# A two-layer linear-attention and MLP block on one core: output tiles in the phi(K) buffers, two more normalised tiles, a last tile cut 384 + 128, and new operation lists

## The chip, the core and the metric

The kernel runs on one NeuronCore of one Trainium2 chip. Five engines work from their own instruction lists: TensorE (PE: matmuls, with the weight loads shown as PEld), VectorE (DVE), ScalarE (ACT), GpSimd (POOL) and SyncE (SP), which here only issues DMAs. They meet through semaphores. The metric is the device time in microseconds; the median of three runs before the change is 328.74 us (328.71 to 331.37).

## The reference

The input x has 2048 tokens of 512 values. Two layers follow each other with the same weights, each with an attention part and an MLP part, and each part is added to its input:

```python
phi = lambda t: jnp.where(t > 0, t + 1, jnp.exp(t)) + 1e-6
# A: H = 32 heads of 16; q, k, v = split(x @ wqkv)
pq, pk = phi(q), phi(k)
kv = jnp.einsum("bhsd,bhse->bhde", pk, v)
z = jnp.einsum("bhsd->bhd", pk)
o = einsum("bhqd,bhde->bhqe", pq, kv) / (einsum("bhqd,bhd->bhq", pq, z)[..., None] + 1e-6)
A = o @ wo
# B: F = 1792
h = gelu(layernorm(x) @ w1 + b1);  B = h @ w2 + b2
...
x = x + A(layernorm(x))
x = x + B(layernorm(x))
x = x + A(layernorm(x))
x = x + B(layernorm(x))
```

The sums kv and z run over all tokens, so the attention output of a layer can't begin before all its keys are there.

## The kernel before

The tokens are 16 tiles of 128 (st 0 to 15), four to a chunk (c 0 to 3). `build_kernel` describes the whole computation as a graph of 1541 named operations, each with an engine, a duration that a planner uses, the tiles it holds, and the function that emits its instructions. The order on each engine is not found by the program: it stands written out in `CONF["ORDER"]`, one list of names for each engine. `Scheduler.run` only walks the five lists with the stated durations, to give every tile a buffer and every operation a place in time; `assign_waits` then derives the semaphore waits. So on the chip each engine runs its list strictly in order, and an operation that waits holds up all behind it on that engine. Constants such as the durations matter only through the buffers they lead to and through the lists that were settled with them.

Names: the layer is L (0 or 1).

- `x0`, `x1`, `x2`, `xc0` to `xc2`: DMAs that load x; `wk0`, `wk1`, `wq`: weights. The first layer begins with chunk 3 (tiles 12 to 15).
- `stats`, `aggr`, `veps`, `pow`, `nmr`, `norm` with A or B, layer and tile (L734 to L774): the layer norm. Statistics are on VectorE, `veps` and `pow` (one over the root) mostly on GpSimd, `norm` on VectorE or ScalarE; the result is a tile of `yb`, of which there are 10. In the first chunk, `cen` subtracts the mean and `ysc` scales later.
- `TA`, `TB` (L784): a DMA transpose of a `yb` tile, issued by SP; `PTA`, `PTB` with `tc` (L797, L807): the same on TensorE, copied out by ScalarE.
- `K`, `Q` (L852, L870, L883): projections. `exp`, `relu`, `min`, `phi` (L822 to L839) turn them into phi(K), in eight buffers `pkb`, and phi(Q). `phi` stands on VectorE or GpSimd.
- `G`, then `ga`, `gt` (L985 to L998): the product of normalised tokens and phi(K), summed over chunks; `KV`, `kvm`, `M`, `cpm` (L1008 to L1031): the value and output weights folded in. `Z`, `zs`, `zb`, `dz`, `ZR`, `D`, `pz`, `red`, `den`, `rec`, `pr` (L934, L1053 to L1085): the denominator. `TP` (L1069) transposes phi(Q) when the denominator is taken token by token.
- `WO` and `RA` (L1101, L1106): attention output and residual; `b2` adds the MLP's bias to it (L1118).
- `W1L_c_f_h` (L1133): the up-projection of chunk c for 128 of the 1792 columns, four matmuls of 512 tokens, or for chunk 0 two halves of 256 (last digit 0 or 1); `gelu` (L1139) on ScalarE.
- `W2L_st_0` and `W2L_st_7` (L1171): the down-projection of a tile in two runs of seven matmuls; `RB` (L1177, L1181) its residual.
- `OD` (L1183): the store of a finished tile, issued by SP. In layer 1 `RB` writes it into one of two `outb` buffers. The last tile (st 15) is cut into two halves of 256 columns, `W21_15_h0` and `h1` (L1158), with `RB1_15_0`, `RB1_15_1` (L1163) and `OD15_0`, `OD15_1` (L1165), so that less is left after the last matmul.
- `warm`, `idle0_0`, `idle0_1` (L690): dummy matmuls at the head, 8 of 512 columns and 1 of 128, then 4 and 3 of 128.

TensorE's eight accumulator banks are shared by all these products; `WO` and `W2` use banks 3, 4 and 5. The tail of the last tile before the change:

```python
ot = Tile(OUT, f"out{st}")
for h in range(2):
    hb = b if h == 0 else Tile(psum, f"w{L}_{st}_h", "w")
    cs = slice(h * D // 2, (h + 1) * D // 2)
```

Of the kernel before, what the change touches and what calls it, by code (L numbers as in the profile page):

```python
# [6 lines left out]
BF16 = mybir.dt.bfloat16  # L7
# [20 lines left out]
DMA_LAT = 800.0  # L28

# [81 lines left out]
class Scheduler:  # L111
# [12 lines left out]
    def run(self):  # L124
# [13 lines left out]
        bus = 0.0  # L138
        for _ in g.ops:
# [33 lines left out]
            if e == "pool" and o.sem is None and o.dur > 300.0:  # L173
                dur += max(0.0, min(dve_busy - at, 400.0))
                pool_busy = at + dur
# [92 lines left out]
def assign_waits(graph, order, sems, dma_sems):  # L268
# [10 lines left out]
    while len(done) < total:  # L279
        moved = False  # L280
        for e in ENGINES:
# [43 lines left out]
    N_WARM2=1, N_IDLE=[4, 3], XQ='sp', WKQ='sp act', WK1=1,  # L325
    LAND={'x0': 3210, 'x1': 3930, 'wk1': 5300, 'wk0': 6430, 'x2': 6950, 'wq': 8450, 'xc0': 9730, 'xc1': 11020, 'xc2': 12240},
# [38 lines left out]
        "act":  # L365
# [167 lines left out]
def build_kernel(nc, A_x, A_wqkv, A_wo, B_x, B_w1, B_b1, B_w2, B_b2, out, conf=None, report=False):  # L533
# [5 lines left out]
    with ExitStack() as es:  # L539
        def SB(name, shape, dt):  # L540
            return es.enter_context(nc.sbuf_tensor(name, shape, dt))
# [46 lines left out]
        def bank(t, n=512):  # L588
            return ps[:, t.slot, 0:n]
# [778 lines left out]
```

## Time and profile before

| what | value |
|---|---|
| runs before | 328.71, 328.74, 331.37 us; median 328.74 |
| the profiled execution's own time, its span | 326.2 us, first to last instruction |
| median less span | 2.5 us |
| granted TensorE clock | 1.000 |
| first projection (K0_12) on TensorE | 6.55 us |
| start of the last matmul | 323.38 us |
| output stores: issue to landing, 128 KB and 64 KB | 2.1 and 2.0 us (medians) |
| DMA transposes of yb: issue to landing | 2.5 us (median, 56 of them) |

The page's first part gives the busy time of each engine and the second the span in 40 slices. The waits are a table of who waited for whom: total, times, longest. The chain is the work that ended last, followed back from the end. In a timeline each line is one or several instructions: start, time from the first start to the last end, engine, line, operation, output and input, count, and in brackets the idle time before it and what ended it. Times on TensorE overlap: a 512-column matmul is shown with 0.38 us but the next one starts 0.216 us after it.

### The profile page before, as it was taken

What the parts mean: (1) busy time and instruction counts of PE and PEld (TensorE: products, weight loads), DVE (VectorE), ACT (ScalarE), POOL (GpSimd) and SP (SyncE); (2) the same over time, 40 slices, a digit from 0 to 9 for tenths busy, and PEclk for the clock granted to TensorE, in tenths of its full rate; (3) what the DMA queues carried; (4) which work ended last, traced back from release to release, by engine and by line L of the source; (5) the groups of instructions that cost most, each with busy time, mean ns of one, the idle gap of its engine ahead of it and who ended that gap; (6) DMA issues with size and microseconds to landing.
All of it is one profiled execution on the core that took longest, in us unless ns stands there. A gap on an engine that the chain in (4) does not pass through costs nothing.

```text
span 326.2 us, 4796 instructions
## 1 busy us (share of the span) xinstructions
PE 320.6 (98%) x1724; PEld 158.2 (48%) x1724; DVE 218.7 (67%) x506; ACT 197.5 (61%) x338; POOL 131.2 (40%) x224
## 2 busy tenths in 40 slices
PE   7999999999999999999999999999999999999996
PEld 3444545656544444444444444458644444444453
DVE  4998689989866662535468899999988663300132
ACT  5998889744753387357963395969923553645200
POOL 3465637673238106134139525645811275100000
PEclk9999999999999999999999999999999999999999
DMA  7424662524012400312110200111153233300011
GB/s 239 163 51 92 173 223 62 181 49 81 21 31 48 97 1 2 74 22 55 27 32 19 47 17 0 28 39 36 32 92 72 48 45 69 81 0 2 32 64 50
DMA packets 47028, 20.39 MB, mean 62 GB/s; under 512 B 41948, under 2 KB 45532, under 8 KB 47004
## 3 DMA queue, kind: packets, MB, share of 16 engines
q1 hardware_dynamic: 45676, 15.09, 20.4%
q0 software_dynamic: 1056, 4.72, 4.5%
q10 hardware_dynamic: 272, 0.26, 0.3%
q8 instruction: 14, 0.23, 0.3%
q14 instruction: 10, 0.08, 0.1%
HBM read 8.00 MB, written 2.10 MB: 31 GB/s over the span
## 4 chain that ended last, share of the span: by engine, by line
PE 91%; DVE 4%; DMA 2%; ACT 1%; SPq 1%; issue 1%; ACTq 0%
PE ps L1133 29%; PE ps L1171 26%; PE ps L1101 9%; PE ps L852 9%; PE ps L870 5%; PE ps L953 4%; PE ps L883 3%; PE ps L985 2%; DMA t<-in_A_x_dram 1%; PE ps L1158 1%; DMA t<-yb 1%; DVE t L839 1%; PE ps L1008 1%; PE ps L1077 1%; PE ps L797 1%
## 5 line engine op out<-in xcount | busy, mean ns | idle before, releaser
L1139 ACT ACTIVATE gT<-ps,b1c 128x512 bf16<-128x512 f32 (+1 forms) x140 | 76.9, 601 | 61.2 <-PE ps L1133 60.8
L1133 PE MATMUL ps<-t,w 128*128 128x512 bf16 (+1 forms) x560 | 102.2, 336 | 0.5 <-DMA t<-yb 0.3
L1171 PE MATMUL ps<-w,gT 128*128 128x512 bf16 x434 | 97.3, 379 | 0.0
L1133 PEld LDWEIGHTS ps<-t,w 128*128 128x128 bf16 x560 | 54.4, 98 | 44.5 <-DMA t<-yb 0.7
L1171 PEld LDWEIGHTS ps<-w,gT 128*128 128x128 bf16 x434 | 42.4, 98 | 50.4 <-ACT gT L1139 0.3
L822 ACT ACTIVATE eb<-ps 128x512 bf16<-128x512 f32 x56 | 32.1, 606 | 21.3 <-PE ps L852 20.3
L749 POOL TENSOR_TENSOR rstd<-veps,neghalf 128x1 f32<-128x1 f32 x64 | 36.7, 581 | 8.2 <-DVE veps L747 5.5
L1181 DVE TENSOR_TENSOR outb<-ps,xsb 128x512 bf16<-128x512 f32 x15 | 10.3, 689 | 40.3 <-PE ps L1171 32.1
L734 DVE BATCH_NORM_STATS2 stats<-xsb 128x6 f32<-128x512 f32 x48 | 32.0, 681 | 0.2
L1101 PE MATMUL ps<-gtb,t 128*128 128x512 bf16 x128 | 31.8, 379 | 0.1
L852 PE MATMUL ps<-wqkv,t 128*128 128x512 bf16 x128 | 31.1, 379 | 0.0
L769 ACT ACTIVATE yb<-xsb,nmr,rstd 128x512 bf16<-128x512 f32 x21 | 16.8, 811 | 12.6 <-POOL nmr L766 12.5
L833 ACT ACTIVATE rb<-ps 128x512 bf16<-128x512 f32 x38 | 22.3, 611 | 1.6 <-PE ps L852 0.9
L739 POOL TENSOR_SCALAR veps<-mv 128x1 f32<-128x1 f32 x32 | 7.3, 227 | 38.4 <-DVE mv L736 36.6
L774 DVE TENSOR_SCALAR yb<-xsb,mv,rstd 128x512 bf16<-128x512 f32 x27 | 15.0, 572 | 9.0 <-POOL rstd L749 8.9
L835 DVE TENSOR_SCALAR eb<-eb 128x512 bf16<-128x512 bf16 x46 | 13.6, 306 | 10.9 <-ACT eb L822 10.8
L1118 POOL TENSOR_TENSOR xsb<-xsb,b2b 128x512 f32<-128x512 f32 x14 | 17.0, 1218 | 8.1 <-DVE yb L774 6.5
L870 PE MATMUL ps<-wqkv,t 128*128 128x512 bf16 x80 | 20.2, 379 | 0.0
L747 POOL TENSOR_SCALAR veps<-mv 128x1 f32<-128x1 f32 x28 | 8.4, 305 | 28.0 <-DVE mv L736 26.9
L1101 PEld LDWEIGHTS ps<-gtb,t 128*128 128x128 bf16 x128 | 12.3, 98 | 14.9 <-ACT gtb L966 0.7
L852 PEld LDWEIGHTS ps<-wqkv,t 128*128 128x128 bf16 x128 | 12.0, 97 | 14.7 <-ACT t L807 0.9
L1065 POOL TENSOR_TENSOR t<-t,rr 128x512 bf16<-128x512 bf16 x7 | 7.7, 1100 | 24.4 <-DVE rr L1061 14.1
(103 smaller groups left out, 398.7 us busy)
## 6 DMA issues: line engine op xcount, KB each, us to landing
w<-in_B_w_dram POOLq DMA_DIRECT2D x4, 896.0 KB, 5.9
out_dram<-outb SPq DMA_DIRECT2D x15, 128.0 KB, 2.1
t<-in_A_x_dram SPq DMA_DIRECT2D x3, 512.0 KB, 7.3
t<-yb SPq DMA_TRANSPOSE x56, 2.5
wqkv<-in_A_wqkv_dram SPq DMA_DIRECT2D x1, 512.0 KB, 5.7
wo<-in_A_wo_dram POOLq DMA_DIRECT2D x1, 512.0 KB, 6.6
wqkv<-in_A_wqkv_dram POOLq DMA_DIRECT2D x1, 512.0 KB, 4.5
t<-t SPq DMA_TRANSPOSE x20, 2.5
```

Of the source, the lines that this page charges most:

```text
L734: G.op("dve", lambda e: e.bn_stats(stats[:, s.slot, :], src()), 620, reads=src_keys, writes=[k + "s"], tiles=[s, *src_tiles], prio=prio, n ...
L749: G.op("pool", lambda e: e.tensor_tensor(rstd[:, s.slot:s.slot + 1], veps[:, s.slot:s.slot + 1], neghalf[:], op=ALU.pow), 570, reads=[k + ...
L769: G.op("act", lambda e: e.activation(yb[:, y.slot, :], src(), ACT.Identity, bias=nmr[:, s.slot:s.slot + 1], scale=rstd[:, s.slot:s.slot + 1]),
L822: G.op("act", lambda e: e.activation(eb[:, et.slot, :], bank(bt), ACT.Exp, scale=factor()), 478, reads=[src_key, *more], writes=[f"e{tag}" ...
L833: G.op("act", lambda e: e.activation(rb[:, rt.slot, :], bank(bt), ACT.Relu, scale=factor()), 478, reads=[src_key, *more], writes=[f"r{tag} ...
L852: ins = e.matmul(bank(b), lhsT=yTa(yT)[:, dt, k * P:(k + 1) * P], rhs=wqkv[:, dt, D:2 * D], start=(dt == 0), stop=(dt == DT - 1))
L870: ins = e.matmul(bank(b), lhsT=yTa(yT)[:, dt, k * P:(k + 1) * P], rhs=wqkv[:, dt, 0:D], start=(dt == 0), stop=(dt == DT - 1))
L1101: ins = e.matmul(bank(wb), lhsT=yTa(pq)[:, kt, k * P:(k + 1) * P], rhs=gtb[:, kt, :], start=(kt == 0), stop=(kt == DT - 1))
L1118: G.op("pool" if on_pool else "dve", lambda e: e.tensor_tensor(xsb[:, st, :], xsb[:, st, :], b2b[:], op=ALU.add), 1120 if on_pool else 600 ...
L1133: ins = e.matmul(bank(b, n), lhsT=w1[:, dt, ft * P:(ft + 1) * P], rhs=yTa(yT)[:, dt, k0 * P:k1 * P], start=(dt == 0), stop=(dt == DT - 1))
L1139: G.op("act", lambda e, ft=ft, b=b, k0=k0, k1=k1, n=n: e.activation(gT[:, g.slot, ft * 512 + k0 * P:ft * 512 + k1 * P], bank(b, n), ACT.Ge ...
L1171: ins = e.matmul(bank(b), lhsT=gT[:, g.slot, ft * 512 + k * P:ft * 512 + (k + 1) * P], rhs=w2[:, ft, :], start=(ft == 0), stop=(ft == FT - 1))
```

## The change

The two `outb` buffers and their pool are gone. Outputs of layer 1 go to the eight `pkb` buffers, which phi(K) no longer needs then, each with its own DMA semaphore. The memory goes to two more `yb` tiles (12). The last tile is cut 384 + 128. The dummies at the head are 8 of 512 and 4 of 128 columns, then 8 and 1 of 128. The planner's durations, its model of VectorE and GpSimd in each other's way, of GpSimd's turn-round and of SP's issue times are replaced, and all five lists are written anew with them; the set of operations and the engine of each are the same. Places differ in 324 of 388 on TensorE, 280 of 323 on ScalarE, 455 of 506 on VectorE, 199 of 220 on GpSimd and 70 of 104 on SP.

```diff
+TAIL = 384
+FORM = {"vepsA": 1, "vepsB": 2, "nmr": 3}
+TURN = ((0.0, 115.0, 115.0, 15.0), (0.0, 0.0, 120.0, 135.0), (0.0, 0.0, 0.0, 15.0), (0.0, 120.0, 120.0, 15.0))
...
+                if e == "sp" and last is not None and o.name[0] == "T" and last.name[0] != "T" and last.nbytes >= 0:
+                    at = max(at, last.start + 620.0)
...
+                if e == "pool" and o.sem is None:
+                    at = max(at, free[e] + TURN[form][FORM.get(o.name[:5], FORM.get(o.name[:3], 0))])
...
-            if o.fast and pool_busy > at:
-                dur += pool_busy - at - 60.0
...
             if o.fast:
+                dur += max(0.0, pool_busy - at - 130.0)
                 dve_busy = at + dur
...
-    N_WARM2=1, N_IDLE=[4, 3], XQ='sp', WKQ='sp act', WK1=1,
+    N_WARM2=4, N_IDLE=[8, 1], XQ='sp', WKQ='sp act', WK1=1,
...
         "pe":
-            "warm PTA0_12 idle0_0 PTA0_13 idle0_1 K0_12 K0_13 PTA0_14 Q0_3_0 Q0_3_2 PTA0_15 K0_14 K0_15 G0_12_0 "
...
-            "KV1_0 KV1_1 Q1_3_1 KV1_2 D1_0_3 Q1_3_2 KV1_3 Q1_2_0 M1_1 M1_0 M1_3 M1_2 Q1_2_1 WO1_0_0 Q1_3_3 WO1_0_1 "
...
-            "W21_9_7 W21_10_0 W21_10_7 W21_8_0 W21_15_h0 W21_8_7 W21_11_0 W21_11_7 W21_15_h1",
+            "warm PTA0_12 idle0_0 PTA0_13 K0_12 idle0_1 K0_13 PTA0_14 Q0_3_0 Q0_3_2 G0_12_0 PTA0_15 K0_14 Q0_3_1 "
...
+            "W10_0_5_0 W10_0_3_0 W10_0_10_0 W10_0_7_0 W10_0_1_0 W10_0_11_1 W10_0_4_1 W10_0_6_1 W20_1_0 W10_0_1_1 "
...
+            "W10_0_3_1 W20_0_7 W20_3_0 W10_0_8_1 W10_0_10_1 W20_2_0 W20_3_7 WO0_12_0 W20_2_7 W10_1_12_0 W10_1_5_0 "
...
+            "Q1_3_1 D1_0_2 D1_0_1 G1_3_0 G1_3_2 G1_2_3 G1_3_3 KV1_0 KV1_1 KV1_2 Q1_3_0 D1_0_3 KV1_3 Q1_2_0 M1_0 "
...
+            "WO1_5_0 WO1_4_0 PTB1_1 Q1_2_3 PTB1_0 WO1_6_0 WO1_7_0 W11_0_8_0 W11_0_10_0 W11_0_6_0 W11_0_0_0 W11_0_7_0 "
...
+            "W11_0_5_1 W11_0_8_1 W11_0_0_1 W21_1_0 W21_1_7 WO1_12_0 W21_2_0 W21_2_7 WO1_14_0 W21_0_0 W21_0_7 W21_3_0 "
...
+            "W11_2_2_0 W21_12_7 W21_8_0 W21_8_7 W21_10_0 W21_10_7 W21_9_0 W21_11_0 W21_9_7 W21_15_h0 W21_11_7 "
+            "W21_15_h1",
...
         "dve":
-            "ones statsA0_12 aggrA0_12 cenA0_12 negA0_13 cenA0_13 vepsA0_12 yscA0_12 statsA0_14 aggrA0_14 cenA0_14 "
...
-            "minq1_0_2 zs1_3 zb1 dz1 minq1_0_3 phiq1_0_2 phiq1_0_1 phiq1_0_3 phiq1_1_3 ga1_2_2 ga1_2_0 red1_1_0 "
-            "gt1_1 den1_1_0 gt1_2 gt1_0 red1_1_1 den1_1_1 ga1_2_3 pz1_1_2 rec1_1_0 gt1_3 red1_1_2 kvm1_0 kvm1_1 "
...
+            "ones statsA0_12 aggrA0_12 cenA0_12 negA0_13 vepsA0_12 cenA0_13 yscA0_12 statsA0_14 aggrA0_14 cenA0_14 "
...
+            "cpg0_3 minq0_2_0 kvm0_1 kvm0_2 kvm0_3 kvm0_0 phiq0_2_0 cpm0_2 pz0_2_0 red0_2_0 RA0_0 statsB0_0 RA0_1 "
+            "aggrB0_0 statsB0_1 aggrB0_1 RA0_3 RA0_2 normB0_1 statsB0_2 normB0_0 RA0_4 RA0_5 aggrB0_2 statsB0_3 "
+            "aggrB0_3 normB0_2 den0_2_0 statsB0_5 RA0_7 normB0_3 pz0_3_0 statsB0_4 rec0_2_0 pz0_3_3 RA0_6 aggrB0_4 "
...
+            "minq1_0_2 minq1_0_3 ga1_2_1 minq1_0_1 zs1_3 dz1 zb1 phiq1_0_2 phiq1_0_1 phiq1_0_3 gt1_1 ga1_2_2 "
+            "minq1_1_3 red1_1_0 ga1_2_0 phiq1_1_3 gt1_0 gt1_2 red1_1_1 ga1_2_3 pz1_1_2 gt1_3 red1_1_2 kvm1_0 kvm1_2 "
...
+            "statsB1_2 aggrB1_2 normB1_0 RA1_3 statsB1_3 RA1_5 aggrB1_3 normB1_2 statsB1_5 RA1_4 normB1_3 minq1_3_2 "
...
+            "RB1_11 RB1_15_1",
         "sp":
-            "TB1_2 TB1_3 TB1_5 TP1_3_1 TB1_4 TB1_7 TB1_6 TP1_3_3 TP1_3_2 OD0 TP1_3_0 TP1_2_0 TP1_2_3 OD3 TP1_2_2 "
-            "OD1 TP1_2_1 TB1_12 TB1_14 OD2 TB1_13 TB1_15 OD4 TB1_11 TB1_9 OD5 TB1_8 TB1_10 OD7 OD14 OD6 OD9 OD12 "
-            "OD13 OD10 OD8 OD15_0 OD11 OD15_1",
...
+            "TP1_3_0 TP1_3_2 TB1_5 TB1_7 TB1_6 TB1_4 OD2 TP1_3_3 TP1_3_1 TP1_2_0 TP1_2_3 TP1_2_2 TP1_2_1 TB1_13 "
+            "TB1_15 TB1_14 TB1_12 TB1_10 TB1_8 TB1_11 OD0 TB1_9 OD4 OD1 OD10 OD5 OD13 OD7 OD9 OD6 OD3 OD8 OD14 OD15_0 "
+            "OD12 OD11 OD15_1",
...
-        NT4, NYB, NPK, NER, NGT, NLR, NSTAT, NOUT = 12, 10, 8, 4, 2, 2, 12, 2
+        NT4, NYB, NPK, NER, NGT, NLR, NSTAT = 12, 12, 8, 4, 2, 2, 12
...
-        outb = SB("outb", [P, NOUT, D], BF16)
...
-                ot = Tile(OUT, f"out{st}")
+                ot = Tile(PK, f"out{st}")
                 for h in range(2):
                     hb = b if h == 0 else Tile(psum, f"w{L}_{st}_h", "w")
-                    cs = slice(h * D // 2, (h + 1) * D // 2)
+                    cs = slice(0, TAIL) if h == 0 else slice(TAIL, D)
+                    n = cs.stop - cs.start
...
-                    G.op("dve", lambda e, hb=hb, cs=cs: e.tensor_tensor(outb[:, ot.slot, cs], bank(hb, D // 2), xsb[:, st, cs], op=ALU.add), 340,
+                    G.op("dve", lambda e, hb=hb, cs=cs, n=n: e.tensor_tensor(pkb[:, ot.slot, cs], bank(hb, n), xsb[:, st, cs], op=ALU.add), 80 + 1.02 * n,
...
-                ot = Tile(OUT, f"out{st}")
-                G.op("dve", lambda e: e.tensor_tensor(outb[:, ot.slot, :], bank(b), xsb[:, st, :], op=ALU.add), 600,
+                ot = Tile(PK, f"out{st}")
+                G.op("dve", lambda e: e.tensor_tensor(pkb[:, ot.slot, :], bank(b), xsb[:, st, :], op=ALU.add), 600,
```

More of the change, by code (lines that the diff above doesn't have):

```diff
@@ L138, in run @@
         bus = 0.0
+        last = None
+        form = 0
         for _ in g.ops:
@@ L167, in run @@
             dur = o.dur
-            if o.fast and pool_busy > at:
-                dur += pool_busy - at - 60.0
+            if e == "sp":
+                if last is not None and o.name[0] == last.name[0] == "T" and at - free[e] < 30.0:
+                    dur += 75.0
+                last = o
+            if e == "pool" and o.sem is None:
+                form = FORM.get(o.name[:5], FORM.get(o.name[:3], 0))
             if o.fast:
+                dur += max(0.0, pool_busy - at - 130.0)
                 dve_busy = at + dur
-            if e == "pool" and o.sem is None and o.dur > 300.0:
-                dur += max(0.0, min(dve_busy - at, 400.0))
-                pool_busy = at + dur
+            if e == "pool" and o.sem is None:
+                dur += max(0.0, dve_busy - at - 130.0)
+                if o.dur > 700.0:
+                    pool_busy = at + dur
             o.dur = dur
@@ L599, in build_kernel @@
         STATS = Pool("stats", NSTAT)
-        OUT = Pool("out", NOUT)
         psum = Banks({
@@ L747, in norm @@
                          lambda e: e.tensor_scalar(veps[:, s.slot:s.slot + 1], mv[:, s.slot, 1:2], EPS, None, op0=ALU.add),
-                         100 if head else 300, reads=[k + "m"], writes=[k + "v"], tiles=[s], prio=prio, name=f"veps{tag}", lat=40)
+                         75 if head else 182, reads=[k + "m"], writes=[k + "v"], tiles=[s], prio=prio, name=f"veps{tag}", lat=50)
             G.op("pool", lambda e: e.tensor_tensor(rstd[:, s.slot:s.slot + 1], veps[:, s.slot:s.slot + 1], neghalf[:], op=ALU.pow),
-                 570, reads=[k + "v", "neghalf"], writes=[k + "r"], tiles=[s], prio=prio, name=f"pow{tag}")
+                 530, reads=[k + "v", "neghalf"], writes=[k + "r"], tiles=[s], prio=prio, name=f"pow{tag}", lat=50)
             if centred:
@@ L767, in norm @@
                                                        op0=ALU.mult, op1=ALU.mult),
-                     330, reads=[k + "r", k + "m"], writes=[k + "n"], tiles=[s], prio=prio, name=f"nmr{tag}")
+                     224, reads=[k + "r", k + "m"], writes=[k + "n"], tiles=[s], prio=prio, name=f"nmr{tag}", lat=45)
                 G.op("act", lambda e: e.activation(yb[:, y.slot, :], src(), ACT.Identity, bias=nmr[:, s.slot:s.slot + 1],
@@ L821, in factor @@
                 return rstd[:, by[0].slot:by[0].slot + 1] if by else 1.0
-            G.op("act", lambda e: e.activation(eb[:, et.slot, :], bank(bt), ACT.Exp, scale=factor()), 478, reads=[src_key, *more], writes=[f"e{tag}"],
+            G.op("act", lambda e: e.activation(eb[:, et.slot, :], bank(bt), ACT.Exp, scale=factor()), 569 if by else 483, reads=[src_key, *more], writes=[f"e{tag}"],
                  tiles=[bt, et, *held], prio=prio, name=f"exp{tag}", lat=90, table="exp")
@@ L826, in phi @@
                 G.op("dve", lambda e: e.tensor_scalar(eb[:, et.slot, :], eb[:, et.slot, :], 1.0, 1e-6, op0=ALU.min, op1=ALU.add),
-                     210, reads=[f"e{tag}"], writes=[f"e{tag}"], tiles=[et], prio=prio, name=f"min{tag}", lat=80, fast=True)
+                     202, reads=[f"e{tag}"], writes=[f"e{tag}"], tiles=[et], prio=prio, name=f"min{tag}", lat=50, fast=True)
                 G.op("dve", lambda e: e.scalar_tensor_tensor(out=dst(), in0=bank(bt), scalar=1.0 + 1e-6, in1=eb[:, et.slot, :],
@@ L832, in phi @@
             rt = Tile(RB, f"r{tag}")
-            G.op("act", lambda e: e.activation(rb[:, rt.slot, :], bank(bt), ACT.Relu, scale=factor()), 478, reads=[src_key, *more], writes=[f"r{tag}"],
+            G.op("act", lambda e: e.activation(rb[:, rt.slot, :], bank(bt), ACT.Relu, scale=factor()), 569 if by else 478, reads=[src_key, *more], writes=[f"r{tag}"],
                  tiles=[bt, rt, *held], prio=prio, name=f"relu{tag}", lat=90)
             G.op("dve", lambda e: e.tensor_scalar(eb[:, et.slot, :], eb[:, et.slot, :], 1.0, 1e-6, op0=ALU.min, op1=ALU.add),
-                 210, reads=[f"e{tag}"], writes=[f"e{tag}"], tiles=[et], prio=prio, name=f"min{tag}", lat=80, fast=True)
+                 202, reads=[f"e{tag}"], writes=[f"e{tag}"], tiles=[et], prio=prio, name=f"min{tag}", lat=50, fast=True)
             on_pool = eng(f"phi{tag}") == "pool"
@@ L1106, in attn_out @@
             G.op("dve", lambda e: e.tensor_tensor(xsb[:, st, :], bank(wb), base(), op=ALU.add), 600,
-                 reads=[f"wo{L}_{st}", *base_keys], writes=[("x", st)], tiles=[wb, *base_tiles], prio=prio, name=f"RA{L}_{st}", lat=40)
+                 reads=[f"wo{L}_{st}", *base_keys], writes=[("x", st)], tiles=[wb, *base_tiles], prio=prio, name=f"RA{L}_{st}", lat=55)
         def mlp_front(L, c, k, yT, prio, on_act):
@@ L1140, in mlp_up @@
                         gT[:, g.slot, ft * 512 + k0 * P:ft * 512 + k1 * P], bank(b, n), ACT.Gelu_apprx_tanh, bias=b1c[:, ft:ft + 1], scale=1.0),
-                        144 + 0.833 * n, reads=[f"h{L}_{c}_{ft}_{hf}", "b1c"], writes=[f"g{L}_{c}_{ft}_{k}" for k in range(k0, k1)],
+                        156 + 0.833 * n, reads=[f"h{L}_{c}_{ft}_{hf}", "b1c"], writes=[f"g{L}_{c}_{ft}_{k}" for k in range(k0, k1)],
                         tiles=[b, g], prio=p, name=f"gelu{L}_{c}_{ft}_{hf}", lat=110, table="gelu")
```

36 lines of the change are left out of this document (18 added, 18 removed), and 247 rows, old and new, of the table ORDER.

## The prediction

> **What bounds the kernel.** I read the page first (busy time, slices, the chain), then the waits of TensorE, then the chain and the timeline around each place where TensorE stops.
>
> ```profile
> PE 320.6 (98%) x1724; PEld 158.2 (48%) x1724; DVE 218.7 (67%) x506; ACT 197.5 (61%) x338; POOL 131.2 (40%) x224
> ...
> PEclk9999999999999999999999999999999999999999
> ...
> PE 91%; DVE 4%; DMA 2%; ACT 1%; SPq 1%; issue 1%; ACTq 0%
> ```
>
> TensorE is the bound: 91% of the chain, at full clock in every slice. A busy share of 98% says little, as ends are modelled, so I take starts. A 512-column matmul starts 216 ns after the one before, a 256-column one 109, a 128-column one 56. Every start from the first projection (K0_12, 6.55 us) on that comes later than this is a stall, and they add up to 2.5 us. No new order can win more than that between 6.55 and the last matmul; what else can move is the head (6.5 us) and the tail (2.8 us from the last matmul's start at 323.38 to the end). The waits of TensorE name the larger ones:
>
> ```profile
> PE ps L797 <- DVE veps L747: 0.9, 1, 0.9
> ...
> PE ps L1008 <- DVE gtb L998: 0.3, 1, 0.3
> PE ps L1133 <- DMA t<-yb: 0.3, 1, 0.3
> PE ps L1133 <- issue: 0.3, 1, 0.3
> ```
>
> Measured by starts, the stalls are: 0.17, 0.06 and 0.19 in the head (8.4 to 11.8 us, ahead of PTA0_14, K0_14 and K0_15); 0.13 and 0.14 at 20.3 and 36.4; 0.41 at 78.8, where the up-projection of chunk 1 begins (W10_1_3_0); 0.43, 0.19 and 0.10 at 203.3, 206.1 and 210.4 (KV1_0, KV1_3, WO1_1_0); 0.28 at 247.0 (WO1_12_0); 0.42 at 272.1, where the up-projection of chunk 3 begins (W11_3_2_0).
>
> **The change part by part.** The sum is made against the profiled span, 326.2 us. The median of the runs is 328.74, so 2.5 us lie outside the span; no edit touches them and I add them back.
>
> *Output tiles in the phi(K) buffers.* Seen from the stall at 272.1:
>
> ```profile
> 264.33 1.17 DVE stats L734 x2
> ...
> 266.75 1.51 SPq L1183
> ...
> 268.31 1.19 SPq L784
> ...
> 269.54 2.49 DMA t<-yb
> ...
> 272.07 1.04 PE ps L1133 x4
> ```
>
> SP issues an output (OD2, 1.51 us) between the second and third of four transposes (TB1_12, 14, 13, 15), and TensorE waits for the fourth to land. With two output buffers the order had to free one there; with eight it need not. The new SP list has TB1_13, 15, 14, 12 in a row, and the output before that chunk's first matmul is OD2, far ahead of them. W11_3 begins at the same place on TensorE, and the four issues are 1.25 us each, so without OD2 the last lands some 1.5 us earlier: -0.42. The stall at 247.0 waits for TP1_3_0, issued behind OD0 (0.58 us); the new list issues TP1_3_0 before both outputs, but WO1_12_0 itself comes 12.5 us earlier on TensorE (sum of matmul times ahead of it), so it could wait again: between -0.28 and +0.3; I take -0.28. VectorE also waited 8.2 us for output DMAs (6.3 and 1.9), but these waits end nothing on TensorE: 0. The extra semaphores that SP waits for at the end are passed while the last output flies (SP idles 1.2 us there): 0.
>
> *Two more normalised tiles.* No wait of TensorE names a missing yb buffer: 0 by itself.
>
> *Order around chunk 0 and 1 of layer 0.* W10_1 now begins 9.5 us later on TensorE and the second half of chunk 0 9.5 us earlier (W10_0_11_1, from 77.5 to 68.0). The first loses the 0.41 at 78.8. The second needs TB0_3 landed by 68.0, which landed at 72.0. Cover: normB0_3 now stands behind 20 VectorE operations after RA0_0 (54.7): seven adds and five statistics at 0.60, the rest small, 9.7 us, so it is done at about 64.5; a transpose lands 2.5 us later, 67.1. That leaves 0.9 us; if it is gone, the price is what is missing. Taken: -0.41.
>
> *The head.* PTA0_13 no longer has three dummies (0.17) between it and K0_12, but vepsA0_12 moves ahead of cenA0_13, which PTA0_13 waits for (0 to 0.1). K0_13 waits for tcA0_13 until 7.23 anyway, and PTA0_14 for the last piece of x (issued 2.19, landing 4.8 later), so at most 0.1 survives. G0_12 and PTA0_15 move ahead of K0_14 and cover the 0.06 and 0.19. The five added dummies (56 ns each, 0.3 us) sit in the waits ahead of PTA0_12 and PTA0_13 (0.4 and 0.9), except one of 56 ns. The clock is already full at 4.57, so they win nothing in this execution. Taken: -0.2 (0 to -0.4).
>
> *KV of layer 1, where VectorE is the limit.* VectorE is busy without a gap over 0.5 us from 185 to 243.
>
> ```profile
> 197.20 2.39 DVE L839 TENSOR_TENSOR t<-eb,rb 128x512 bf16<-128x512 bf16 x4
> ...
> 198.15 1.16 POOL L1053 TENSOR_TENSOR lr<-t,zrow 128x512 f32<-128x512 bf16 x1 [3.55 <-ACT zrow L966]
> ...
> 203.32 0.62 PE L1008 MATMUL ps<-gtb,wqkv 128*128 128x128 bf16 x8 [0.27 <-DVE gtb L998]
> ```
>
> Four short additions at L839 took 2.39 us. Three are normal (0.42); the fourth, phiq1_1_3, took 1.38 and ended with the GpSimd operation beside it: a hold of 0.96. The new list has 0.73 us less VectorE work ahead of gt1_0 (gt1_2 and a small one move behind), so KV1_0's 0.43 goes. But KV1_3 stands 0.86 earlier while gt1_3 has only 0.52 less ahead: it ends at 205.55 where TensorE, unstalled, would be there at 204.65. What is late next is WO1_7_0, which needs RA1_5's bank (218.3 by the same count, against 217.4). So the section loses 0.9 if the hold stays and nothing if it goes, against 0.72 before. Taken: 0 (-0.7 to +0.3).
>
> *The last tile, 384 + 128 columns.*
>
> ```profile
> 321.96 1.69 PE L1158 MATMUL ps<-w,gT 128*128 128x256 bf16 x14
> 322.31 0.69 DVE L1181 TENSOR_TENSOR outb<-ps,xsb 128x512 bf16<-128x512 f32 x1 [2.48 <-DMA out_dram<-outb]
> 323.03 0.33 SPq L1183 DMA_DIRECT2D out_dram<-outb  x1
> 323.69 0.43 DVE L1163 TENSOR_TENSOR outb<-ps,xsb 128x256 bf16<-128x256 f32 x1 [0.69 <-PE ps L1158]
> 324.14 0.33 SPq L1165 DMA_DIRECT2D out_dram<-outb  x1
> ```
>
> TensorE's sum is unchanged (14 x 109 twice; now 14 x 162 and 14 x 56). Call E the end of the last matmul's stream (323.49). Before, the last add started at E+0.20 and the last output was issued at E+0.65. By the rows 0.69 for 512 columns and 0.43 for 256, 128 take about 0.29. But the last stretch is now 0.78 long instead of 1.53, so RB1_11 starts at E-0.43 and occupies VectorE to E+0.2, its output is issued at E+0.29, and SP takes the next one 0.37 later (312.29, 312.66). The last output is issued at E+0.66: nothing won. An output issued right behind another took 0.43 three times and 1.20 once (OD15_0, landing 2.5 against 1.6): 0 to +0.9, I take 0, the commoner row.
>
> Here a page speaks against the change. The rows give 56 ns for 128-column matmuls that each load weights (KV1_1: 56, 55, 56). The Trainium skill, "TensorE: Matmul & The Clock Gate", section "Back-to-back issue gap", gives about 81 ns for such a sustained stream; by it the last 14 would end 0.35 us later. I go by the row. "DMA: Bandwidth & Descriptors", section "Specifications", says pieces under 512 B fall below line rate because the engine reads, modifies and writes; no output row here is that short (512 and 1,024 B), and the last one becomes 256 B.
>
> *Everything else in the lists.* 324 of 388 places on TensorE hold another operation. Slack between producer and TensorE is often 0.2 us in the old order (the gelu stretches), so new small stalls are likely: bounds 0 and the 2.5 us of the old lists together; I take +0.3, as ten operations at 0.03, the small W10 row at 63.6.
>
> Sum: -0.42 -0.28 -0.41 -0.2 +0 +0 +0.3 = -1.0. Span 325.2, time 327.7.
>
> **The rivals.** (1) *Even* (328.4 to 329.1): VectorE's stretch takes back what the stalls give, or the order does not do what it says and the transposes land late anyway. For: VectorE has no gap there. Against: three of the removed stalls lie outside it. (2) *Slower by the hold on VectorE*: minq1_1_3 and phiq1_1_3 now stand where GpSimd runs pr1_0_0 and pz1_1_1 back to back. Each hold costs up to 0.96, and with no gap until 243 it reaches TensorE whole. Beyond one more hold the gain is spent; two more give -1.0 + 1.9 = +0.9, 329.6. Against: seven of the short operations at these lines that met a long GpSimd one were not held. (3) *A slow last output* of 256 B rows: +0.9, 328.6; it falls into the even case. (4) *All stalls go*: 2.5 less, 326.2.
>
> **How the numbers follow.** Forecast (326.7 to 328.3) 0.60; even 0.17; slower by more than 0.4 us 0.18, of which 0.05 by over 1% (a transpose chain late by several us); nearly all stalls gone 0.05. The range 326.4 to 329.7 leaves out the far slow end and the last 0.2 of the good one. One per cent, 3.3 us, is about what a measurement tells from no change, and more than all stalls together: faster by over 1% needs head and tail too, 0.03; slower 0.05; within 0.92.
>
> **What would show it.** Right: no TensorE wait for a transpose near 79 and 272; stalls by starts near 1.5 us in all; the last output issued 0.6 to 0.7 after the last matmul. Wrong: waits of L1008 or L1101 over 1 us between 200 and 222; a short L835 or L839 operation over 1 us there; W10_0_11_1 waiting at 68; the last output landing after more than 2 us.

## The result, and the profile after

The changed kernel takes 326.59 us (median, 326.32 to 327.09); the kernel before takes 328.75 beside it (328.25 to 331.37). The ratio is 0.9917, interval 0.9891 to 0.9943: faster by 0.6 to 1.1%, or 2.2 us between the medians, where 1.0 was forecast. The medians of the kernel before swing from 328.02 to 328.75 between sets of runs; beside 328.36 the changed kernel took 326.59 again, 1.8 less. The span of the profiled execution falls from 326.2 to 324.6.

The page of the changed kernel, busy time, clock and chain:

```profile
PE 320.2 (99%) x1729; PEld 159.6 (49%) x1729; DVE 216.6 (67%) x506; ACT 197.2 (61%) x338; POOL 132.3 (41%) x224
...
PEclk9999999999999999999999999999999999999999
...
PE 96%; DMA 2%; SPq 1%; issue 0%; DVE 0%
```

TensorE was 91% of the chain and is now 96%; VectorE's 4% are gone. The waits of TensorE, longest first (us in total, times, longest), are a list of two:

```profile
PE ps L700 <- PEq L1364: 0.8, 1, 0.8
PE ps L880 <- DMA wqkv<-in_A_wqkv_dram: 0.2, 1, 0.2
```

The first is the start of the program. The second is Q0_3_0 waiting for its weights at 8.7 us. No wait for a transpose, for `gtb` or for an accumulator is left. By starts, TensorE's lateness between K0_12 and the last matmul (the time between the two starts, less what the matmuls between them take) falls from 2.50 us to 0.51. The late starts read one by one, as in the table below, add up to 2.55 and 0.59, and all but 0.02 of the latter lie before 9 us (K0_13 0.21, Q0_3_0 0.36). So nearly all stalls went, the case that the prediction had given 1 chance in 20. This is the account of the span, from the two traces:

| place | before | after | difference | forecast |
|---|---|---|---|---|
| head: K0_12's start, late starts to 12 us, a dummy moved behind K0_12 | 6.55 + 0.42 | 6.12 + 0.57 + 0.06 | -0.22 | -0.2 |
| 20.3, 36.4, 63.6 ("everything else") | 0.30 | 0 | -0.30 | +0.3 |
| 78.8, up-projection of chunk 1 | 0.41 | 0 | -0.41 | -0.41 |
| 203 to 217, KV of layer 1 | 0.72 | 0.02 | -0.70 | 0 |
| 247.0, WO1_12_0 | 0.28 | 0 | -0.28 | -0.28 |
| 272.1, up-projection of chunk 3 | 0.42 | 0 | -0.42 | -0.42 |
| tail, from E (end of the last matmul's stream) | 2.73 | 3.47 | +0.74 | 0 |
| sum | | | -1.6 | -1.0 |

Three rows are far off in size: KV by 0.70 and "everything else" by 0.60 to the good, the tail by 0.74 to the bad. That the tail takes back one of the others is luck.

*KV.* The stretch in which phiq1_1_3 was held, VectorE and then GpSimd (start, duration, operation; in brackets, in later rows, the idle time before it and what ended it):

```profile
199.42 0.41 DVE L849 TENSOR_TENSOR t<-eb,rb 128x512 bf16<-128x512 bf16 x1
199.75 1.36 DVE L1008 TENSOR_TENSOR gtb<-ps,gacc 128x512 bf16<-128x512 f32 x2
...
199.48 1.37 POOL L1063 TENSOR_TENSOR lr<-t,zrow 128x512 f32<-128x512 bf16 x1
```

The operation took 0.41 us in place of 1.38. It began 0.06 before GpSimd's operation, and now that one is longer (1.37 where its neighbours take 1.16). gt1_3 (the last L1008 row of the section) begins at 202.82 where it began at 205.44, and TensorE comes to KV1_3 at 203.70.

*Tail.* SP's issues at the end, and the rows of the two store lines there (min/median/max of the issue in ns):

```profile
312.94 7.82 SPq L1194 DMA_DIRECT2D out_dram<-pkb  x9
320.80 0.45 SPq L1176 DMA_DIRECT2D out_dram<-pkb  x1
321.29 0.93 SPq L1194 DMA_DIRECT2D out_dram<-pkb  x2
322.27 0.45 SPq L1176 DMA_DIRECT2D out_dram<-pkb  x1
```

```profile
L1194 SPq DMA_DIRECT2D out_dram<-pkb x7: 333/441/1457, 317.5 to 321.8; - x7
L1176 SPq DMA_DIRECT2D out_dram<-pkb x2: 445/447/449, 320.8 to 322.3; - x2
```

The add of the last 128 columns ended at 321.62, as the rows had said. Its store was issued only at 322.27, E+1.15: SP was working off a queue. In the new list OD10, whose tile is ready at 312.9, stands ahead of seven tiles that were ready between 248 and 307; they leave behind it, one each 0.49 us, and one of them, OD3, took 1.46.

### The profile page after: what moved, and what is told of

It reads as the page before. It is cut to its first block, busy times and chain, and to the rows that moved or that the text cites. A ratio compares the mean times of both kernels' runs of the same rounds, so it can differ in the third digit from the quotient of the medians.

```text
span 324.6 us, 4788 instructions
## 1 busy us (share of the span) xinstructions
PE 320.2 (99%) x1729; PEld 159.6 (49%) x1729; DVE 216.6 (67%) x506; ACT 197.2 (61%) x338; POOL 132.3 (41%) x224
## 4 chain that ended last, share of the span: by engine, by line
PE 96%; DMA 2%; SPq 1%; issue 0%; DVE 0%
PE ps L1143 30%; PE ps L1182 29%; PE ps L1111 9%; PE ps L862 8%; PE ps L880 5%; PE ps L963 4%; PE ps L995 4%; PE ps L893 3%; DMA wqkv<-in_A_wqkv_dram 2%; PE ps L1169 1%; PE ps L1087 1%; PE ps L944 1%; PE ps L1018 1%; PE ps L1041 1%; PE ps L807 0%; SPq L660 0%
## 5 line engine op out<-in xcount | busy, mean ns | idle before, releaser
L1192 DVE TENSOR_TENSOR pkb<-ps,xsb 128x512 bf16<-128x512 f32 x15 | 10.1, 681 | 39.4 <-PE ps L1182 37.5
L1111 PE MATMUL ps<-gtb,t 128*128 128x512 bf16 x128 | 31.1, 379 | 0.0
L845 DVE TENSOR_SCALAR eb<-eb 128x512 bf16<-128x512 bf16 x46 | 14.7, 329 | 21.3 <-ACT eb L832 21.2
L749 POOL TENSOR_SCALAR veps<-mv 128x1 f32<-128x1 f32 x32 | 8.2, 256 | 36.7 <-DVE mv L746 34.9
L963 PE MATMUL ps<-pkb,yb 128*128 128x512 bf16 x64 | 15.8, 379 | 0.0
```

What stands on the lines that cost most here:

```text
L963: ins = e.matmul(ps[:, gb.slot + dc, :], lhsT=yb[:, y.slot, dc * P:(dc + 1) * P], rhs=pkb[:, pk.slot, :], start=(st == FIRST), stop=(st == ...
L1111: ins = e.matmul(bank(wb), lhsT=yTa(pq)[:, kt, k * P:(k + 1) * P], rhs=gtb[:, kt, :], start=(kt == 0), stop=(kt == DT - 1))
```

## The experiments

All were run beside the kernel before, in three sets; its median in them was 328.36 (the changed kernel again, ready order, 256 + 256, the hold put back), 328.02 (fewer dummies, the first move of phiq1_1_3, the moved store, the buffers) and 328.15 (the rest). Medians from different sets can therefore differ by some 0.3 us by themselves. "Late" is the sum of TensorE's late starts from K0_12 on. Each difference in trace places comes from one profiled execution.

### The changed kernel again

> The changed kernel once more, as the reference for the variants beside it. Both theories: 326.3 to 327.1 us, some 2.1 us under the kernel before; TensorE's late starts from K0_12 to the last matmul 0.5 us in all; the last store issued 1.15 us after the last matmul's stream ends.

Measured: 326.59 (326.15 to 328.68), ratio 0.9941 (0.9921 to 0.9960). Late 0.14, so even the 0.36 at Q0_3_0 is not in every execution. The tail is worse in this profile:

```profile
L1194 SPq DMA_DIRECT2D out_dram<-pkb x7: 332/438/2177, 317.5 to 322.6; - x7
```

OD3 took 2.18 us, the last store left at E+1.85, and the core ended 4.17 after E. A long issue pushes everything behind it.

### Stores of layer 1 in the order in which they are ready

```diff
-TB1_11 OD0 TB1_9 OD4 OD1 OD10 OD5 OD13 OD7 OD9 OD6 OD3 OD8 OD14 OD15_0 OD12 OD11 OD15_1
+TB1_11 OD0 TB1_9 OD4 OD1 OD3 OD5 OD7 OD6 OD14 OD13 OD12 OD10 OD8 OD9 OD15_0 OD11 OD15_1
```

> The changed kernel with the stores of layer 1 issued in the order in which their tiles are ready (OD3, OD5, OD7, OD6, OD14, OD13 and OD12 go ahead of OD10). Theory 1, SP's queue of back-to-back stores sets the tail: nine issues at 0.49 us no longer stand behind OD10, the last store is issued at 0.52 after the last matmul in place of 1.15, so 0.5 to 0.7 us less, about 326.0. Theory 2, the short rows of the last store set it: the last issue comes earlier but its landing stays, or the total stays within 0.2 us.

Measured: 325.45 (325.13 to 325.50), ratio 0.9896 (0.9870 to 0.9922): 1.14 below the changed kernel, and below both kernels. SP's last issues:

```profile
317.33 0.33 SPq L1194 DMA_DIRECT2D out_dram<-pkb  x1
319.47 0.33 SPq L1176 DMA_DIRECT2D out_dram<-pkb  x1
321.12 0.33 SPq L1194 DMA_DIRECT2D out_dram<-pkb  x1
321.50 0.42 SPq L1176 DMA_DIRECT2D out_dram<-pkb  x1
```

The queue is gone, the last store leaves at E+0.52 and lands 1.7 later. So with the stores in this order the tail is short again; the gain is more than the 0.5 that I had read from one profile, since the long issue had fallen into the queue.

### The last tile cut 256 + 256 again

```diff
-TAIL = 384
+TAIL = 256
```

> The changed kernel with the last tile cut 256 + 256 as before, lists as they are. Theory 1 (SP's queue sets the tail): the last add ends 0.14 us later, still ahead of SP, so the last store is issued at the same 1.15 us after the last matmul: same within 0.2 us. Theory 2 (256 B rows cost): the landing falls from 1.8 to 1.6 us or less, 0.2 us or more gained.

Measured: 326.57 (325.69 to 327.40), the changed kernel's time, so by the medians the cut makes no difference here. But it is not as theory 1 had it: in the profiled execution no issue was long and SP's queue had run dry, so that the last store left at E+0.65 and not at E+1.15, and still the core ended 4.20 after E. The DMA queues from 321.7 on (packets, MB, share), and the issues there (KB each, median us to landing):

```profile
q8 instruction: 1, 0.02, 2.0%
...
out_dram<-pkb SPq DMA_DIRECT2D x1, 64.0 KB, 3.1
```

A 16 KB packet of the instruction queue q8 ran at 322.25 for 1.36 us, while the last store was on its way, and the store took 3.1 to land in place of some 2. OD3's long issue could have the same neighbour.

### Fewer dummies at the head

```diff
-N_WARM2=4, N_IDLE=[8, 1]
+N_WARM2=1, N_IDLE=[4, 1]
```

> The changed kernel with the dummies at the head cut again (N_WARM2 4 to 1, N_IDLE 8 and 1 to 4 and 1). My step (the added dummies sit in waits and the clock is full anyway) expects a time within 0.2 of the changed kernel without this edit, and K0_12 at 6.1 to 6.6. The rival (they keep the clock open or open it earlier) expects the first projections at half rate for some tenths of a us longer: 128-column matmuls 107 ns apart instead of 56 until past 6 us, and 0.3 to 1.0 more than the changed kernel.

Measured: 325.63 (325.21 to 326.66), ratio 0.9921 (0.9894 to 0.9948): some 0.9 below the changed kernel (0.2 to 0.6 when each is set against the kernel before in its own set), which neither side had expected. In this profile the clock opened late (512-column matmuls 0.43 and 0.36 apart at 5.9 and 6.4), and yet K0_12 came at 5.94 and the last matmul 0.24 earlier than in the changed kernel. The rest, 0.65, is the tail:

```profile
317.24 2.29 SPq L1194 DMA_DIRECT2D out_dram<-pkb  x5
319.56 0.45 SPq L1176 DMA_DIRECT2D out_dram<-pkb  x1
320.05 1.30 SPq L1194 DMA_DIRECT2D out_dram<-pkb  x2
321.41 0.42 SPq L1176 DMA_DIRECT2D out_dram<-pkb  x1
```

SP's queue is the changed kernel's, but no issue took more than 0.46, so it had run dry at 320.50, 0.5 us before the store ahead of the last was ready. There is no q8 packet after 300 us in this trace. In the changed kernel there is one at 318.47, for 1.07 us, inside OD3's 318.33 to 319.79; in its second profile one at 318.57 for 1.61, inside OD3's 318.38 to 320.56.

### Both at once, and the middle number of dummies

The stores in ready order together with the fewer dummies; and the changed kernel with N_IDLE=[4, 1] alone.

> The changed kernel with the stores of layer 1 in the order in which they are ready, and with the fewer dummies. Theory (both edits won their 1 us by the same thing, the store that is issued beside the 16 KB block of instructions at 318.5 and holds up SP): no store of over 0.5 us at the end, last store at 0.5 to 0.6 behind E, and a time within 0.3 of the store order alone (325.1 to 325.7). Rival (the dummies cost 0.9 at the head by themselves): the gains add up, 324.3 to 324.8.

Measured: 325.68 (325.46 to 326.43), ratio 0.9929 (0.9914 to 0.9943). The gains do not add up. In the traces the reason is that with either edit the tail is mended, and with both there is nothing left to mend: it is 2.73 long here, 2.74 with the store order alone. The time by itself would not settle it, for in this profile K0_12 came 0.45 earlier than with the store order alone, and TensorE then waited 0.4 at 130.5 (W10_3_11_0) for a gelu to read a bank, which it did not there:

```profile
PE ps L1143 <- ACT gT L1149: 0.4, 1, 0.4
```

> The changed kernel with four dummies fewer in the head (N_IDLE 8 to 4, N_WARM2 left at 4). It tells whether the long store follows the block of instructions: TensorE has 8 instructions fewer, so the block that it fetched at 318.5 should come some 1 us later. Theory: the long issue (1.5 to 2.4 us) leaves OD3 for the store being issued then, or is gone with the block; never a store over 1 us without a block beside it. Rival (OD3 is long by itself, being the first store behind a stretch of idle, or of its data): OD3 takes 1.4 to 2.4 us again whatever the block does. Time 325.5 if the block misses the stores, 326.6 if it meets one.

Measured: 325.84 (325.09 to 327.66), ratio 0.9936 (0.9913 to 0.9960). No q8 packet after 300 us, OD3 takes 0.45, the last store leaves at E+0.52. So OD3 is not long by itself.

These five kernels are a table of two causes. In each cell stands where the last store left, when the core ended (both from E), and the median time:

| | q8 packet at 318.4 to 318.6 | no q8 packet after 300 |
|---|---|---|
| seven old stores queued behind OD10 | E+1.15, E+3.47 and E+1.85, E+4.17; 326.59 | E+0.52, E+2.82; 325.63 and E+0.52, E+2.81; 325.84 |
| stores in ready order | E+0.52, E+2.74; 325.45 | E+0.52, E+2.73; 325.68 |

In these profiles neither the queue nor the packet alone makes the tail more than 0.1 longer; where they meet, it is 0.7 to 1.4 longer. The packets and the places are those of one execution each (of two for the changed kernel), the times medians over executions of which most have no trace. And a packet alone is not harmless wherever it falls: with 256 + 256 above it came later, beside the last store, and no queue was needed to make the tail 4.20. The two q8 rows, of the changed kernel's second profile and of the ready order, between 318 and 320:

```profile
q8 instruction: 1, 0.02, 5.0%
```

```profile
q8 instruction: 1, 0.02, 4.4%
```

The ends of the issues say more than their meeting. Over all fourteen profiles, behind 100 us, twelve stores took more than 0.6 us to issue. All twelve began between 0.22 before and 0.27 after the start of a q8 packet, and eleven ended 0.37 to 0.38 after the packet did, whatever its length (the twelfth, the changed kernel's OD3, 0.25): in the changed kernel's second profile the packet ended at 320.18 and OD3 at 320.56; in the kernel before 321.06 and 321.43 for OD15_0 (the issue of 1.20 that the prediction had shown). So these issues ended with the packet, not with anything of their own; through what SP waits for it, no run shows. OD2 in the kernel before, whose 1.51 us held up the transposes at 272, is another of the twelve: packet 266.49 to 267.89, issue to 268.26. Not every store near a packet is held: in the run with the moved store, OD8 began 0.16 before one and took 0.33. In the ready order SP issued nothing from 317.66 to 319.47 and the packet ran from 318.40 to 319.81; the store of 319.47, begun in its last third, took the usual 0.33. The one cost there is that the store of 317.33 landed after 3.7, and nobody waits for that.

The Trainium skill, "Runtime: NRT & Kernel Launch", section "Instruction fetch mechanics", says that each engine fetches its instructions in blocks of 16 KiB, 256 instructions, over a DMA queue of its own, and calls the cost mostly hidden. The trace agrees on the blocks: 14 q8 packets of 16 KB for TensorE's 3,458 matmuls and weight loads. It does not agree that a block is as good as free: the stores that were held beside one took 1.2 to 2.4 us to issue in place of 0.33 to 0.46.

What stays open: why the last packet is absent with fewer dummies, and also in the next kernel, whose TensorE list is as long as the changed kernel's.

### Ready order with the last tile cut 256 + 256

> The changed kernel with the stores of layer 1 in ready order and the last tile cut 256 + 256 as before, so that SP's queue is empty when the last store comes. My step (by the rows the last store is issued at E+0.65 with 256 columns; with 384 + 128 it was issued at E+0.58 in that order) expects 0.1 more than the store order alone. If rows of 256 B land slower, as the Trainium skill has it for short pieces (DMA: Bandwidth & Descriptors, Specifications), the landing after 384 + 128 (1.7 there) is the longer one and the cut of 256 wins 0.1 to 0.9. If the cut is what the edit promises, the halves cost 0.2 to 0.5 more.

Measured: 326.58, but the executions fall apart: 325.11 and 325.55, and four from 326.56 to 327.46. The ratio is 0.9946 (0.9924 to 0.9967). The profiled one is of the first kind, without a q8 packet at the end: last store at E+0.66, landing 1.6, end at E+2.72, against E+0.52, 1.7 and E+2.74 with 384 + 128. So in the two profiles the cut is worth nothing: 384 + 128 won 0.14 at the issue and lost 0.15 at the landing (0.09 of it because that store's own issue was longer, 0.42 against 0.33). By the medians, though, this kernel is 1.1 slower than the same order cut 384 + 128, whose six executions all lie within 0.4. The four slower ones have no trace; that the packet met the last store in them, as in the other kernel cut 256 + 256, is likely and not shown. What the cut is worth over many executions therefore stays open.

### The hold, put where it was

The changed kernel with minq1_1_3 and phiq1_1_3 ahead of gt1_1:

```diff
-phiq1_0_3 gt1_1 ga1_2_2 minq1_1_3 red1_1_0 ga1_2_0 phiq1_1_3 gt1_0
+phiq1_0_3 minq1_1_3 phiq1_1_3 gt1_1 ga1_2_2 red1_1_0 ga1_2_0 gt1_0
```

> The changed kernel with minq1_1_3 and phiq1_1_3 back ahead of gt1_1, where GpSimd starts pz1_1_0. The same VectorE work stands ahead of gt1_3. Theory 1 (the hold of a short VectorE addition by a GpSimd operation makes the KV stall): one of the two takes about 1.0 us more, gt1_3 ends 0.9 later, TensorE waits 0.6 to 0.9 us around KV1_0, KV1_3 and WO1_7_0, and the time grows by as much, about 327.3. Theory 2 (it was the amount of VectorE work ahead of the gt operations): no more than 0.2 us.

Measured: 332.6 (331.93 to 333.82), ratio 1.0118 (1.0090 to 1.0145).

```profile
197.69 1.33 DVE L849 TENSOR_TENSOR t<-eb,rb 128x512 bf16<-128x512 bf16 x1
...
197.59 1.15 POOL L1063 TENSOR_TENSOR lr<-t,zrow 128x512 f32<-128x512 bf16 x1 [4.04 <-ACT zrow L976]
```

```profile
PE ps L1143 <- ACT gT L1149: 1.1, 2, 0.6
...
PE ps L1018 <- DVE gtb L1008: 0.7, 1, 0.7
PE ps L1143 <- DVE xsb L1116: 0.5, 1, 0.5
```

The hold came back as made to (1.33 in place of 0.41), and KV1_3 and WO1_0_0 are late by 0.89 and 0.47. But over 4 us more were lost at the first up-projections of layer 1, where no operation was moved. The program's own walk of the lists gave 70 accumulator tiles another bank, and TensorE now waits for banks to be read. So this run shows the hold, and can't price it. The next two are moves that change the place of few tiles.

### One move that gets rid of the hold, and what it meets

The kernel before, with phiq1_1_3 behind gt1_0 (10 tiles change place):

> The kernel before with one VectorE operation moved: phiq1_1_3 (128x512 bf16, 1.38 us where 0.42 is its time without GpSimd beside it) goes behind gt1_0, out of the way of GpSimd's pz1_1_1. The same work stays ahead of gt1_3. Theory (the hold is the whole of the section's lateness): phiq1_1_3 takes 0.42 to 0.5, gt1_0 ends 1.2 to 1.4 earlier and gt1_3 0.8 to 1.0 earlier, the late starts at KV1_0, KV1_3 and WO1_1_0 (0.43, 0.19, 0.10) go, time 0.6 to 0.7 below before. Rival (the amount of VectorE work sets the section, another short operation is held instead): late starts there of 0.5 or more and a time within 0.2 of before.

Measured: 329.15 (328.57 to 329.82), ratio 1.0024 (1.0009 to 1.0039): slower by 0.3 to 1.3.

```profile
202.33 1.22 DVE L839 TENSOR_TENSOR t<-eb,rb 128x512 bf16<-128x512 bf16 x1
...
204.87 1.57 DVE L1053 TENSOR_TENSOR lr<-t,zrow 128x512 f32<-128x512 bf16 x1
...
202.10 1.17 POOL L1085 TENSOR_TENSOR t<-t,lr 128x512 bf16<-128x512 bf16 x1
...
204.73 1.17 POOL L1085 TENSOR_TENSOR t<-t,lr 128x512 bf16<-128x512 bf16 x1 [1.46 <-ACT lr L1081]
```

phiq1_1_3 met the next operation of GpSimd and was held again, and pz1_1_2 behind it, 0.68 long in the kernel before, met the one after that and took 1.57. KV1_0's lateness is gone, as gt1_0 had no hold ahead of it; KV1_3 is late by 1.45. Theory and rival were both half right: the hold sets the section, and it is given to whichever short operation is there.

So phiq1_1_3 went two operations further (2 tiles change place):

```diff
-phiq1_0_3 phiq1_1_3 ga1_2_2 ... gt1_0 red1_1_1 den1_1_1 ga1_2_3
+phiq1_0_3 ga1_2_2 ... gt1_0 red1_1_1 den1_1_1 phiq1_1_3 ga1_2_3
```

> The kernel before with phiq1_1_3 moved past den1_1_1, 0.9 us further than where it was held the second time. Theory (the hold by GpSimd is the whole lateness of the section): by the trace of the first move the operation comes up some 0.14 before GpSimd's operation there ends, and pz1_1_2 behind it finds GpSimd idle; so no short VectorE operation over 0.6 us between 197 and 207, no late start at KV1_0 and KV1_3 (0.62 before), time 0.6 to 0.8 below before. If one of the two is held again, late starts of 0.4 to 0.8 there, in step with the hold. Rival (VectorE's work sets the section and the hold is beside the point): no hold, and still 0.4 or more late at KV1_3, time within 0.2 of before.

Measured: 327.67 (327.16 to 328.74), ratio 0.9989 (0.9978 to 1.0000).

```profile
202.79 0.41 DVE L839 TENSOR_TENSOR t<-eb,rb 128x512 bf16<-128x512 bf16 x1
...
203.73 0.68 DVE L1053 TENSOR_TENSOR lr<-t,zrow 128x512 f32<-128x512 bf16 x1
...
201.67 1.17 POOL L1085 TENSOR_TENSOR t<-t,lr 128x512 bf16<-128x512 bf16 x1
...
204.03 1.40 POOL L1085 TENSOR_TENSOR t<-t,lr 128x512 bf16<-128x512 bf16 x1 [1.19 <-ACT lr L1081]
```

No hold on VectorE, and neither KV1_0 nor KV1_3 is late; 0.22 came up at WO1_0_0. So late starts from KV1_0 to WO1_7_0 follow the holds: none and 0.02 in the changed kernel, none and 0.22 here, one and 0.72 before, two and 1.45. The time fell by 0.5 (0 to 0.7 by the interval), 0.1 to 0.3 short of expected; the late starts at WO1_12_0, which swing between 0 and 0.62 in the profiles of the old lists, were at 0.62 here.

The rows also show who wins. Where VectorE's operation began first (199.42 against 199.48, 203.73 against 204.03), it kept its time and GpSimd's grew by 0.2; where GpSimd's began first, VectorE's ended 0.3 to 0.5 after it. The operations at L835 and L839 that met a 128x512 operation of GpSimd in the profile before and kept their time fit this: they began 0.08 to 0.28 before it, or in its last 0.15. The Trainium skill, "SBUF — State Buffer", section "SBUF: two separate sides", has this as a rule: the two share one pair of ports, and the operation that starts first has it for its whole length. The rows agree. What the hold costs is therefore set by who comes first, and 0.1 us of order can decide about 0.9.

### One store moved, and the buffers without the lists

The kernel before with OD2 behind the fourth transpose:

```diff
-TB1_12 TB1_14 OD2 TB1_13 TB1_15 OD4
+TB1_12 TB1_14 TB1_13 TB1_15 OD2 OD4
```

> The kernel before with one issue moved: output OD2 goes behind TB1_13 and TB1_15 in SP's list, so that the four transposes of chunk 3 are issued in a row, as in the changed kernel. My step (the 0.42 at W11_3_2_0 goes, and nothing is late next) expects no TensorE wait at the up-projection of chunk 3, late starts of TensorE down by 0.4 (2.5 to about 2.1) and a time 0.4 lower than before. The rival (output buffers: with two of them a later output now waits for OD2's to come free, and VectorE or SP hands the 0.42 on) expects late starts of 2.4 to 2.6 with a new place behind 275, and a time within 0.1 of before.

Measured: 327.66 (327.11 to 328.07), ratio 0.9985 (0.9970 to 1.0001), by the time alone not clear of no change. SP issues now run as four transposes and then the outputs:

```profile
263.89 5.92 SPq L784 DMA_TRANSPOSE t<-yb  x4
269.85 3.25 SPq L1183 DMA_DIRECT2D out_dram<-outb  x2
```

The stall at 272 is gone, and nothing behind 275 is late in its place: late 2.34, of which about 1.0 lies before 22 us in this execution. The last matmul comes 0.75 earlier than before, with the stall at 247 gone too, which nothing here was meant to touch. So two `outb` buffers were enough for this order, and the 0.42 was the list's, not the buffers'.

The kernel before with its old lists, outputs in the phi(K) buffers and twelve normalised tiles:

```diff
-NT4, NYB, NPK, NER, NGT, NLR, NSTAT, NOUT = 12, 10, 8, 4, 2, 2, 12, 2
+NT4, NYB, NPK, NER, NGT, NLR, NSTAT = 12, 12, 8, 4, 2, 2, 12
-ot = Tile(OUT, f"out{st}")
+ot = Tile(PK, f"out{st}")
```

> The kernel before, with its old lists, but with the outputs in the phi(K) buffers (two output buffers to eight) and twelve normalised tiles in place of ten. Theory: buffers by themselves are worth nothing, since every order was written for the old ones; time within 0.3 of before (328.4), the wait of VectorE for output DMAs (8.2 in all) gone, TensorE's late starts 2.2 to 2.8. Rival (the buffers carry the gain: the order of before was waiting for them): late starts under 1.5, time 1 or more below before. The walk that assigns buffers and PSUM banks gives 84 tiles another place with these counts; stalls that come from that would show as TensorE waits that name a PSUM reader (ACT or DVE), not a transpose.

Measured: 328.87 (328.20 to 330.23), ratio 1.0023 (1.0007 to 1.0040): slower by 0.2 to 1.3. TensorE's waits:

```profile
PE ps L1169 <- DVE pkb L1179: 0.8, 1, 0.8
...
PE ps L1131 <- DMA t<-yb: 0.3, 1, 0.3
PE ps L1006 <- DVE gtb L996: 0.3, 1, 0.3
PE ps L1099 <- DMA t<-t: 0.3, 1, 0.3
```

VectorE's waits for output DMAs are gone, as they should be, and the old stalls are all there. One new wait of 0.8 names a reader of an accumulator (W21_13_0 at 305.9): the tiles have other banks. The buffers are worth nothing without lists written for them. The other way round, the new lists can't be walked with ten normalised tiles: the program finds no free one for TA1_15. So the tiles are a condition of the gain and not its source.

## Why the prediction was wrong, and where it was right

The kernel took 326.59 where 327.7 (326.7 to 328.3) was forecast: the gain is twice the forecast one. What bounds the kernel, and the three stalls that would go, were right. Four terms of the sum failed: KV, taken at 0, was -0.70; "everything else", taken at +0.3, was -0.30; the 2.5 us outside the span were 1.75; and the tail, taken at 0, was +0.74. The first three point the same way, and only the tail, a miss of its own, kept the forecast within 1.1.

- **TensorE as the bound, and the stalls as the most that can be won**: right. 1.99 of 2.50 went. The case "all stalls go" was worked out at 326.2; the time came 0.4 above it, with the tail's 0.74 to the bad.
- **The stalls at 272, 247 and 78.8** (-0.42, -0.28, -0.41): right, each gone and none replaced. The moved store alone brought the first. The price that I had set beside the third, TB0_3 landing too late, did not come: normB0_3 was done at 64.30 where 64.5 was counted, TB0_3 landed at 66.74, and W10_0_11_1 began unstalled at 67.46.
- **The head** (-0.2): right, -0.22, though K0_12's start swings between 5.9 and 7.2 over the profiles, more than that. The step "the clock is full at 4.57, so the dummies win nothing in this execution" holds for that execution alone: full rate began anywhere between 3.7 and 6.6 us, with many dummies or few.
- **KV of layer 1** (taken 0): wrong in size, by 0.70. The mechanism was right: hold stays, loses 0.9; hold goes, loses nothing, against 0.72 before. That is a choice between +0.2 and -0.7, and I put it at a middle that neither branch gives. In the new order phiq1_1_3 came up 0.06 before GpSimd's operation. The rival "slower by the hold" has its mechanism confirmed, by the run with two holds, and did not happen.
- **The tail** (0 to +0.9, taken 0): wrong in size, +0.74. The step that failed is "its output is issued at E+0.29, and SP takes the next one 0.37 later": I counted one store ahead of the last, where eight stand in an unbroken row. The lists showed it: seven tiles done by 307 stand behind OD10, done at 312.9. By itself that row ends in time, 0.5 before the store ahead of the last is ready; one issue held by a packet, 1.0 to 1.7 longer, uses that up. I had the held issue in view (the 1.20), gave it a chance and no cause, and the row to push not at all. Without the row the last store left at E+0.52, 0.14 earlier than counted. The 128-column rows were right: 0.29 for the add, and 56 ns for a matmul that loads its own weights. Fourteen of them:

```profile
320.34 0.94 PE L1169 MATMUL ps<-w,gT 128*128 128x128 bf16 x14
```

  Their starts are 55 to 56 ns apart. The 81 ns of the Trainium skill ("TensorE: Matmul & The Clock Gate", "Back-to-back issue gap"), which would have added 0.35, are not seen. Nor do 256 B rows land late: 1.75 us after an issue of 0.45 began, against 1.80 for the 512 B rows of OD15_0, issued in 0.44, in the kernel cut 256 + 256. So the rival "a slow last output" falls, and the loss at its place has another cause.
- **Everything else** (+0.3): wrong, -0.30. Behind 9 us no new stall over 0.02 came in this profile, with 324 changed places, and three old ones of 0.13, 0.14 and 0.03 went. The chance of small new stalls was real all the same: in four profiles of the variants W10_3_11_0 at 130.5 was late by 0.05 to 0.4.
- **2.5 us outside the span**: wrong, by 0.75, as large a part of the miss as any. I took the profiled span from the median of other runs. With each run set against its own span, 1.7 to 1.9 us lie outside in 167 of 171 runs (2.0 to 2.9 in the other four), 1.75 at the median, before and after alike. The profiled execution of before took about 328.0, so 0.7 of the forecast time was the difference of two executions, and the forecast should have been 327.0.

## What to carry to other kernels

Where a hold goes to whoever comes first, price the two branches and choose one: the middle is the one value that can't come out. Before a last store is priced, work off its queue by hand: for each store ahead of it on the issuing engine the time when its tile is ready, so that none stands behind a younger one; here that order was worth 1.1 us, half as much as the whole change. And an order is written for one assignment of buffers and banks: compare the assignment when one operation is moved, or the run measures something else.

## What the runs showed of the hardware that I had not expected

- Twelve stores that SP began to issue within 0.3 us of the start of a 16 KB packet of the instruction queue took 1.2 to 2.4 us in place of 0.33 to 0.46, and eleven of them ended 0.37 us after the packet. Of the transposes beside one, 30 of 51 ended 0.41 to 0.44 after it. Stores already under way beside one took up to 4.2 us to land in place of about 2.
- Stores issued back to back cost SP 0.49 us each, those after a pause 0.33 and the next 0.43.
- A short VectorE operation on `eb`, `rb` or `lr` that began in the first quarter of a 128x512 GpSimd one took 0.8 to 1.0 longer and ended 0.15 to 0.55 after it; one that began up to 0.3 before it was not slowed, and GpSimd's took 0.2 longer.
- TensorE's full rate at the head began anywhere between 3.7 and 6.6 us after the start, at both ends of this with the same dummies (3.7 with the store order and fewer dummies, 6.6 with fewer dummies alone).
